# GQA decode attention: K transposes moved from TensorE to VectorE, a wide V accumulator, and load shapes that differ between the kv heads

## The chip, the cores and the metric

One core of a Trainium2 chip runs the whole program. The metric is the time of one execution on the device in microseconds (us). "The span" is the time from the first to the last instruction in a profiled execution. It is about 2 us shorter than the time.

Every run carries a state: fast, or slow when it lies over 1.5% above the fastest of the same kernel. One of the first two runs of the kernel before (745.04 us) was a slow one.

## The reference

```python
B, Hq, Hkv, Sq, Sk, D = 1, 32, 8, 1, 65536, 128      # bf16; q, k, v = normal * 0.05
k = jnp.repeat(k, Hq // Hkv, axis=1); v = jnp.repeat(v, Hq // Hkv, axis=1)
scores = jnp.einsum("bhqd,bhkd->bhqk", q, k) * D ** -0.5
out = jnp.einsum("bhqk,bhkd->bhqd", softmax(scores, -1), v)
```

There is one query token, 32 query heads, and 8 kv heads with 65536 keys each. K and V together are 268.4 MB and each byte is needed once. A kv head is 33.55 MB: four 4 MB K blocks and four 4 MB V blocks of 16384 keys.

## The kernel before

The scores need the head dimension on the partitions, but K arrives with the keys there. So each 128x128 chunk of K is transposed on TensorE into PSUM, copied to SBUF by VectorE, and used as the stationary operand of a matmul whose moving operand is four query columns. V needs no transpose: a V chunk is the stationary operand, and four columns of probabilities move.

```python
# io pool: 4 buffers of 4 MB, shared by K and V; all loads issued from SyncE
nc.sync.dma_start(out=kn, in_=k[0, g, block].rearrange("(c p t) d -> p c t d", p=P, t=32))  # 8 KB runs
# K step, a group of NW = 8 chunks
for i in range(NW):
    nc.tensor.transpose(out=pt[:, i*P:(i+1)*P], in_=kn[:, c, t0+i, :], identity=ident_bf)
nc.vector.tensor_copy(out=kTn, in_=pt)                       # 128x1024 bf16, PSUM -> SBUF
for i in range(NW):
    nc.tensor.matmul(out=sc[:, jj*4:(jj+1)*4], lhsT=kTn[:, i*P:(i+1)*P], rhs=qT_g)
# ... per head: max, exp on ScalarE, sum ...
# V step, one matmul for each chunk
nc.tensor.matmul(out=psum_oT, lhsT=vb[:, c, t, :], rhs=E_g[:, j*4:(j+1)*4])
# main loop: K groups of head g+1 alternate with V chunks of head g  [cut]
```

Of the kernel before, what the change touches and what calls it, by code (L numbers as in the profile page):

```python
# [13 lines left out]
IO_BUFS = int(os.environ.get("GQA_IOBUFS", "4"))  # L14
PTW = int(os.environ.get("GQA_PTW", "8"))
SBUFS = int(os.environ.get("GQA_SBUFS", "3"))
EBUFS = int(os.environ.get("GQA_EBUFS", "4"))
GRAN = int(os.environ.get("GQA_GRAN", "8"))
# [3 lines left out]
def kernel(  # L22
# [8 lines left out]
    P = nc.NUM_PARTITIONS  # L31
    B, Hq, Sq, D = q.shape
    _, Hkv, Sk, _ = k.shape
    assert B == 1 and Sq == 1 and D == P
    HPG = Hq // Hkv
    assert HPG * Hkv == Hq
    assert Sk % P == 0
    C = Sk // P
    SCALE = float(D) ** -0.5

    fp32 = mybir.dt.float32
    bf16 = mybir.dt.bfloat16

    KB = min(Sk, 16384)
    assert Sk % KB == 0
    NB = Sk // KB
    T = 32 if KB >= 32 * P else 1
    CB = KB // (P * T)
    CKB = KB // P
    assert CKB * HPG <= 512  # L50
    NW = PTW if T % PTW == 0 else 4
    assert CKB % GRAN == 0 and GRAN % NW == 0

    const = ctx.enter_context(tc.tile_pool(name="const", bufs=1))
    iopool = ctx.enter_context(tc.tile_pool(name="iopool", bufs=IO_BUFS))
    ktp = ctx.enter_context(tc.tile_pool(name="ktp", bufs=3))
    spool = ctx.enter_context(tc.tile_pool(name="spool", bufs=SBUFS))
    epool = ctx.enter_context(tc.tile_pool(name="epool", bufs=EBUFS))
    stats = ctx.enter_context(tc.tile_pool(name="stats", bufs=2))
    psc = ctx.enter_context(tc.tile_pool(name="psc", bufs=2, space=bass.MemoryType.PSUM))  # L60
    pst = ctx.enter_context(tc.tile_pool(name="pst", bufs=2, space=bass.MemoryType.PSUM))
    psm = ctx.enter_context(tc.tile_pool(name="psm", bufs=2, space=bass.MemoryType.PSUM))
    pso = ctx.enter_context(tc.tile_pool(name="pso", bufs=2, space=bass.MemoryType.PSUM))

    qT = const.tile([P, Hq], bf16)
    nc.sync.dma_start_transpose(out=qT[:, :], in_=q[0, :, 0, :])  # L66

    ident = const.tile([P, P], fp32)
    make_identity(nc, ident[:, :])
    ident_bf = const.tile([P, P], bf16)  # L70
    nc.vector.tensor_copy(out=ident_bf[:, :], in_=ident[:, :])
    ones_row = const.tile([1, P], fp32)
    nc.vector.memset(ones_row[:, :], 1.0)
    ones_mat = const.tile([P, P], fp32)
    nc.gpsimd.memset(ones_mat[:, :], 1.0)
    lsum_all = const.tile([P, Hq], fp32)
    rl_all = const.tile([P, Hq], fp32)
    oT_all = const.tile([P, Hq], bf16)

    E_tiles = [None] * Hkv  # L80
    S_tiles = [None] * Hkv
    psum_oTs = [None] * Hkv

    def stats_and_exp(g):
        S_g = S_tiles[g]
        S_view = S_g[:, :].rearrange("p (c h) -> p h c", h=HPG)
        mx = stats.tile([P, HPG], fp32, name="mx")
        nc.vector.tensor_reduce(out=mx[:, :], in_=S_view, axis=AX.X, op=ALU.max)  # L88
        psum_t = psm.tile([HPG, P], fp32, name="psum_t", tag="misc")
        nc.tensor.transpose(out=psum_t[:, :], in_=mx[:, :], identity=ident[:, :])  # L90
        m4 = stats.tile([HPG, 1], fp32, name="m4")
        nc.vector.reduce_max(out=m4[:, :], in_=psum_t[:, :], axis=AX.X)
        psum_mrow = psm.tile([1, HPG], fp32, name="psum_mrow", tag="misc")
        nc.tensor.transpose(out=psum_mrow[:, :], in_=m4[:, :], identity=ident[:HPG, :HPG])  # L94
        mrow = stats.tile([1, HPG], fp32, name="mrow")
        nc.vector.tensor_copy(out=mrow[:, :], in_=psum_mrow[:, :])  # L96
        psum_b = psm.tile([P, HPG], fp32, name="psum_b", tag="misc")
        nc.tensor.matmul(  # L98
            out=psum_b[:, :], lhsT=ones_row[:, :], rhs=mrow[:, :], start=True, stop=True
        )  # L100
        nmb = stats.tile([P, HPG], fp32, name="nmb")
        nc.vector.tensor_scalar_mul(out=nmb[:, :], in0=psum_b[:, :], scalar1=-SCALE)  # L102
        E_g = epool.tile([P, C * HPG], bf16, name="E_g")
        E_view = E_g[:, :].rearrange("p (c h) -> p h c", h=HPG)
        for h in range(HPG):
            nc.scalar.activation(  # L106
                out=E_view[:, h, :],
                in_=S_view[:, h, :],
                func=ACT.Exp,
                bias=nmb[:, h:h + 1],  # L110
                scale=SCALE,
                accum_out=lsum_all[:, g * HPG + h:g * HPG + h + 1],
            )
        E_tiles[g] = E_g
        psum_lb = psm.tile([P, HPG], fp32, name="psum_lb", tag="misc")
        nc.tensor.matmul(  # L116
            out=psum_lb[:, :],
            lhsT=ones_mat[:, :],
            rhs=lsum_all[:, g * HPG:(g + 1) * HPG],
            start=True,  # L120
            stop=True,
        )
        nc.vector.reciprocal(out=rl_all[:, g * HPG:(g + 1) * HPG], in_=psum_lb[:, :])  # L123

    class KBlock:
        def __init__(self, g, b):
            self.g = g
            self.b = b
            self.kn = iopool.tile([P, CB, T, D], bf16, name="kn", tag="io")
            nc.sync.dma_start(  # L130
                out=self.kn[:, :, :, :],
                in_=k[0, g, b * KB:(b + 1) * KB, :].rearrange("(c p t) d -> p c t d", p=P, t=T),
            )
            self.sc = psc.tile([P, CKB * HPG], fp32, name="sc")
            self.done = 0

        def step(self, nchunks):
            g = self.g
            qT_g = qT[:, g * HPG:(g + 1) * HPG]
            end = min(self.done + nchunks, CKB)  # L140
            while self.done < end:
                g0 = self.done
                c = g0 // T
                t0 = g0 % T
                pt = pst.tile([P, NW * P], bf16, name="pt")
                for i in range(NW):
                    t = t0 + i
                    nc.tensor.transpose(  # L148
                        out=pt[:, i * P:(i + 1) * P],
                        in_=self.kn[:, c, t, :],  # L150
                        identity=ident_bf[:, :],
                    )
                kTn = ktp.tile([P, NW * P], bf16, name="kTn")
                nc.vector.tensor_copy(out=kTn[:, :], in_=pt[:, :])  # L154
                for i in range(NW):
                    jj = g0 + i
                    nc.tensor.matmul(  # L157
                        out=self.sc[:, jj * HPG:(jj + 1) * HPG],
                        lhsT=kTn[:, i * P:(i + 1) * P],
                        rhs=qT_g,  # L160
                        start=True,
                        stop=True,
                    )
                self.done += NW
            if self.done >= CKB:
                S_g = S_tiles[g]
                c0 = self.b * CKB * HPG
                nc.vector.tensor_copy(out=S_g[:, c0:c0 + CKB * HPG], in_=self.sc[:, :])  # L168
                return True
            return False  # L170

    class VBlock:
        def __init__(self, g, b):
            self.g = g
            self.b = b
            self.vb = iopool.tile([P, CB, T, D], bf16, name="vb", tag="io")
            nc.sync.dma_start(
                out=self.vb[:, :, :, :],
                in_=v[0, g, b * KB:(b + 1) * KB, :].rearrange("(c p t) d -> p c t d", p=P, t=T),
            )  # L180
            if psum_oTs[g] is None:
                psum_oTs[g] = pso.tile([P, HPG], fp32, name="psum_oT")
            self.done = 0

        def step(self, nchunks):
            g = self.g
            E_g = E_tiles[g]
            psum_oT = psum_oTs[g]
            end = min(self.done + nchunks, CKB)
            while self.done < end:  # L190
                jj = self.done
                c = jj // T
                t = jj % T
                j = self.b * CKB + jj
                nc.tensor.matmul(  # L195
                    out=psum_oT[:, :],
                    lhsT=self.vb[:, c, t, :],
                    rhs=E_g[:, j * HPG:(j + 1) * HPG],
                    start=(j == 0),
                    stop=(j == C - 1),  # L200
                )
                self.done += 1
            if self.done >= CKB:
                if self.b == NB - 1:
# [5 lines left out]
                    )  # L210
                return True
            return False

    for g in range(Hkv):
        S_tiles[g] = spool.tile([P, C * HPG], bf16, name="S_g")

# [64 lines left out]
```

## Time and profile before

| Reading | Value | View |
|---|---|---|
| time, fast runs | about 708 us | run list |
| bytes from HBM at 426 GB/s, the rate of the best 20 us windows | 268.4 MB / 426 GB/s = 630 us | table by stage |
| one kv head, steady state | 87.8 us (382 GB/s) | packet records of the trace |
| TensorE | 12337 matmuls, 562 us busy | page, part 1 |

Lines of the page of the kernel before: busy time by engine; the span in 40 slices (digits are tenths busy, for PE and for DMA, then the rate of DMA); the chain of work that ended last; and the costliest groups (busy us, mean ns of one | idle time just before, and its releaser).

```profile
PE 562.4 (80%) x12337; PEld 505.3 (72%) x12337; DVE 396.7 (56%) x595; ACT 41.9 (6%) x65; POOL 0.8 (0%) x7
...
PE   1998898839988499884999849998498984999945
...
DMA  8999799997989979899799997989979899799994
GB/s 332 427 425 425 305 405 387 386 426 327 423 356 391 426 319 425 353 397 421 308 423 377 404 420 321 423 358 425 427 309 408 360 393 423 325 413 386 425 427 202
...
PE 67%; DVE 20%; issue 6%; ACT 5%; DMA 2%; SPq 0%; DVEq 0%; ACTq 0%
PE pt L148 34%; PE sc L157 17%; DVE kTn L154 15%; PE psum_oT L195 15%; ACT E_g L106 5%; DVE mx L88 3%; DMA kn<-in_k_dram 2%; DVE S_g L168 1%; PE psum_b L98 1%; PE psum_lb L116 1%; PE psum_t L90 0%; PE psum_mrow L94 0%; DVE nmb L102 0%; SPq 
...
L154 DVE COPY kTn<-pt 128x1024 bf16<-128x1024 bf16 x512 | 350.0, 691 | 223.1 <-PE pt L148 214.8
L148 PE MATMUL pt<-ident_bf,kn 128*128 128x128 bf16 x4096 | 367.5, 244 | 14.5 <-DMA kn<-in_k_dram 14.5
...
L157 PE MATMUL sc<-qT,kTn 128*128 128x4 bf16 x4096 | 184.1, 167 | 33.8 <-DVE kTn L154 18.2
...
L195 PE MATMUL psum_oT<-E_g,vb 128*128 128x4 bf16 x4096 | 118.7, 166 | 26.8 <-issue 26.8
```

The rate holds at 425 to 427 GB/s in the good slices and falls to between 305 and 327 in one slice of each head. The loads are the same in every slice, so the likely reading is that the stream is starved; experiment 1 tests it. The chain consists of TensorE and of the VectorE evictions between its transposes; DMA is 2% of it. Note that VectorE is idle for 223 us before the evictions, nearly all of it waiting for the PE transposes.

Table by stage, two windows of 20 us of the kernel before (columns: window, length, busy us of PE, PEld, DVE, ACT, POOL, then granted clock, DMA share, GB/s):

```profile
40.00:60.00 20.00, 17.89 (x392) 15.81 (x390) 17.24 (x27) 0.00 (x0) 0.00 (x0) 1.00 1.01 424
80.00:100.00 20.00, 18.89 (x420) 17.39 (x418) 13.38 (x22) 0.69 (x2) 0.00 (x0) 0.83 0.74 300
```

The first window is saturated (DMA share 1.01) while head 0 fills the buffers. In the second, TensorE is busy 18.89 of 20 us and DMA only 0.74. What the load queue waits for, in total over the span (us, times, longest):

```profile
SPq L130 <- PE psum_oT L195: 369.4, 20, 19.8
SPq L130 <- PE pt L148: 175.0, 8, 25.2
```

Loads wait for buffers that TensorE has not finished with. Two successive lines of the VectorE timeline in head 0 (start, busy us, of two groups each) give the pace of K work:

```profile
61.25 1.34 DVE L154 COPY kTn<-pt 128x1024 bf16<-128x1024 bf16 x2 [0.27 <-PE pt L148]
62.86 1.34 DVE L154 COPY kTn<-pt 128x1024 bf16<-128x1024 bf16 x2 [0.27 <-PE pt L148]
```

Two groups of eight chunks take 62.86 - 61.25 = 1.61 us, so a block of 16 groups takes 12.9 us, while a 4 MB block arrives in 9.8 us. From head 1 on, V work and the softmax come on top. In the timeline of VectorE, line L168 is the copy that closes a K block; here it is from the second block of one head to the second block of the next:

```profile
198.00 0.69 DVE L168 CAST S_g<-sc 128x512 bf16<-128x512 f32 x1 [0.47 <-PE sc L157]
218.02 0.69 DVE L168 CAST S_g<-sc 128x512 bf16<-128x512 f32 x1 [0.47 <-PE sc L157]
237.35 0.69 DVE L168 CAST S_g<-sc 128x512 bf16<-128x512 f32 x1 [0.40 <-PE sc L157]
263.24 0.69 DVE L168 CAST S_g<-sc 128x512 bf16<-128x512 f32 x1 [0.45 <-PE sc L157]
286.16 0.69 DVE L168 CAST S_g<-sc 128x512 bf16<-128x512 f32 x1 [0.47 <-PE sc L157]
```

One head takes 286.16 - 198.00 = 88.2 us, longer than the 78.7 us that its bytes need. Little of that is waiting for data: the K transposes waited 14.5 us for DMA in the whole span (line L148 above). The longest step, 25.9 us, contains the softmax. Two lines of the TensorE timeline show its end:

```profile
247.58 0.59 PE L116 MATMUL psum_lb<-lsum_all,ones_mat 128*128 128x4 f32 x2 [5.43 <-ACT E_g L106]
248.02 1.87 PE L148 MATMUL pt<-ident_bf,kn 128*128 128x128 bf16 x16
```

From the last scores (237.3 us) to the next K transposes (248.02 us) TensorE stands almost idle for 10.7 us; one head earlier it is 10.6 us (149.6 to 160.2 us).

### The profile page before, as it was taken

What the parts mean: (1) busy time and instruction counts of PE and PEld (TensorE: products, weight loads), DVE (VectorE), ACT (ScalarE), POOL (GpSimd) and SP (SyncE); (2) the same over time, 40 slices, a digit from 0 to 9 for tenths busy, and PEclk for the clock granted to TensorE, in tenths of its full rate; (3) what the DMA queues carried; (4) which work ended last, traced back from release to release, by engine and by line L of the source; (5) the groups of instructions that cost most, each with busy time, mean ns of one, the idle gap of its engine ahead of it and who ended that gap; (6) DMA issues with size and microseconds to landing.
All of it is one profiled execution on the core that took longest, in us unless ns stands there. A gap on an engine that the chain in (4) does not pass through costs nothing.

```text
span 705.8 us, 26009 instructions
## 1 busy us (share of the span) xinstructions
PE 562.4 (80%) x12337; PEld 505.3 (72%) x12337; DVE 396.7 (56%) x595; ACT 41.9 (6%) x65; POOL 0.8 (0%) x7
## 2 busy tenths in 40 slices
PE   1998898839988499884999849998498984999945
PEld 1777887738877388773888738888387873888845
DVE  1888666536565365653656536566265662656620
ACT  0000200020000200002000020000200002000020
POOL 0000000000000000000000000000000000000000
PEclk9999788868988678876788768788578885789755
DMA  8999799997989979899799997989979899799994
GB/s 332 427 425 425 305 405 387 386 426 327 423 356 391 426 319 425 353 397 421 308 423 377 404 420 321 423 358 425 427 309 408 360 393 423 325 413 386 425 427 202
DMA packets 34011, 270.12 MB, mean 383 GB/s; under 512 B 1136, under 2 KB 1136, under 8 KB 1136
## 3 DMA queue, kind: packets, MB, share of 16 engines
q1 hardware_dynamic: 33904, 268.46, 91.9%
q8 instruction: 96, 1.57, 0.8%
q14 instruction: 11, 0.09, 0.0%
HBM read 268.44 MB, written 0.01 MB: 380 GB/s over the span
## 4 chain that ended last, share of the span: by engine, by line
PE 67%; DVE 20%; issue 6%; ACT 5%; DMA 2%; SPq 0%; DVEq 0%; ACTq 0%
PE pt L148 34%; PE sc L157 17%; DVE kTn L154 15%; PE psum_oT L195 15%; ACT E_g L106 5%; DVE mx L88 3%; DMA kn<-in_k_dram 2%; DVE S_g L168 1%; PE psum_b L98 1%; PE psum_lb L116 1%; PE psum_t L90 0%; PE psum_mrow L94 0%; DVE nmb L102 0%; SPq L66 0%; DVE mrow L96 0%
## 5 line engine op out<-in xcount | busy, mean ns | idle before, releaser
L154 DVE COPY kTn<-pt 128x1024 bf16<-128x1024 bf16 x512 | 350.0, 691 | 223.1 <-PE pt L148 214.8
L148 PE MATMUL pt<-ident_bf,kn 128*128 128x128 bf16 x4096 | 367.5, 244 | 14.5 <-DMA kn<-in_k_dram 14.5
L148 PEld LDWEIGHTS <-kn 128*128 128x128 bf16 x4096 | 281.6, 109 | 14.5 <-DMA kn<-in_k_dram 14.5
L157 PE MATMUL sc<-qT,kTn 128*128 128x4 bf16 x4096 | 184.1, 167 | 33.8 <-DVE kTn L154 18.2
L157 PEld LDWEIGHTS <-kTn 128*128 128x128 bf16 x4096 | 145.8, 99 | 84.2 <-DVE kTn L154 75.9
L195 PE MATMUL psum_oT<-E_g,vb 128*128 128x4 bf16 x4096 | 118.7, 166 | 26.8 <-issue 26.8
L195 PEld LDWEIGHTS <-vb 128*128 128x128 bf16 x4096 | 114.2, 99 | 28.8 <-issue 28.8
L106 ACT ACTIVATE E_g<-S_g,nmb 128x512 bf16<-128x512 bf16 x32 | 40.6, 1416 | 641.0 <-DVE nmb L102 641.0
L116 PE MATMUL psum_lb<-lsum_all,ones_mat 128*128 128x4 f32 x16 | 4.4, 349 | 37.9 <-ACT E_g L106 37.9
L116 PEld LDWEIGHTS psum_lb<-lsum_all,ones_mat 128*128 128x128 f32 x16 | 3.8, 295 | 38.6 <-ACT E_g L106 38.6
L168 DVE CAST S_g<-sc 128x512 bf16<-128x512 f32 x32 | 22.1, 690 | 12.5 <-PE sc L157 12.5
L123 DVE RECIPROCAL rl_all<-psum_lb 128x4 f32<-128x4 f32 x8 | 1.5, 181 | 40.5 <-PE psum_lb L116 40.5
L90 PE MATMUL psum_t<-ident,mx 128*4 128x128 f32 x8 | 2.9, 360 | 23.2 <-DVE mx L88 23.2
L88 DVE TENSOR_REDUCE mx<-S_g 128x4 f32<-128x2048 bf16 x8 | 18.3, 2284 | 0.2
L90 PEld LDWEIGHTS psum_t<-ident,mx 128*4 128x4 f32 x8 | 0.6, 81 | 23.9 <-DVE mx L88 22.3
L205 DVE TENSOR_TENSOR oT_all<-psum_oT,rl_all 128x4 bf16<-128x4 f32 x8 | 1.2, 153 | 18.1 <-PE psum_oT L195 18.1
L106 ACT ACTIVATION_READ_ACCUMULATOR E_g<-S_g,nmb 128x1 f32 x32 | 8.0, 251 | 0.0
L98 PE MATMUL psum_b<-mrow,ones_row 1*128 1x4 f32 x16 | 4.7, 361 | 1.7 <-DVE mrow L96 1.7
L98 PEld LDWEIGHTS psum_b<-mrow,ones_row 1*128 1x128 f32 x16 | 4.0, 308 | 2.4 <-DVE mrow L96 2.3
L102 DVE TENSOR_SCALAR nmb<-psum_b 128x4 f32<-128x4 f32 x8 | 1.3, 163 | 5.3 <-PE psum_b L98 5.2
L96 DVE COPY mrow<-psum_mrow 1x4 f32<-1x4 f32 x8 | 1.2, 150 | 1.9 <-PE psum_mrow L94 1.8
L106 ACT ACT_TABLE_LOAD x1 | 1.3, 1283 | 0.7 <-PEq L265 0.7
(36 smaller groups left out, 6.2 us busy)
## 6 DMA issues: line engine op xcount, KB each, us to landing
kn<-in_k_dram SPq DMA_DIRECT2D x32, 4096.0 KB, 14.0
vb<-in_v_dram SPq DMA_DIRECT2D x32, 4096.0 KB, 23.1
qT<-in_q_dram SPq DMA_TRANSPOSE x1, 2.3
out_dram<-o_sb SPq DMA_DIRECT2D x1, 8.0 KB, 1.4
```

What stands on the lines that cost most here:

```text
L88: nc.vector.tensor_reduce(out=mx[:, :], in_=S_view, axis=AX.X, op=ALU.max)
L90: nc.tensor.transpose(out=psum_t[:, :], in_=mx[:, :], identity=ident[:, :])
L98: nc.tensor.matmul(out=psum_b[:, :], lhsT=ones_row[:, :], rhs=mrow[:, :], start=True, stop=True)
L102: nc.vector.tensor_scalar_mul(out=nmb[:, :], in0=psum_b[:, :], scalar1=-SCALE)
L106: nc.scalar.activation(out=E_view[:, h, :], in_=S_view[:, h, :], func=ACT.Exp, bias=nmb[:, h:h + 1], scale=SCALE, accum_out=lsum_all[:, g ...
L116: nc.tensor.matmul(out=psum_lb[:, :], lhsT=ones_mat[:, :], rhs=lsum_all[:, g * HPG:(g + 1) * HPG], start=True, stop=True,)
L123: nc.vector.reciprocal(out=rl_all[:, g * HPG:(g + 1) * HPG], in_=psum_lb[:, :])
L148: nc.tensor.transpose(out=pt[:, i * P:(i + 1) * P], in_=self.kn[:, c, t, :], identity=ident_bf[:, :],)
L154: nc.vector.tensor_copy(out=kTn[:, :], in_=pt[:, :])
L157: nc.tensor.matmul(out=self.sc[:, jj * HPG:(jj + 1) * HPG], lhsT=kTn[:, i * P:(i + 1) * P], rhs=qT_g, start=True, stop=True,)
L168: nc.vector.tensor_copy(out=S_g[:, c0:c0 + CKB * HPG], in_=self.sc[:, :])
L195: nc.tensor.matmul(out=psum_oT[:, :], lhsT=self.vb[:, c, t, :], rhs=E_g[:, j * HPG:(j + 1) * HPG], start=(j == 0), stop=(j == C - 1),)
```

## The change

VectorE transposes K directly from SBUF to SBUF, as pairs: two adjacent bf16 are seen as one 32-bit word, and 128x2048 words are transposed in 32x32 squares. The odd layout that results is absorbed in the stationary operand, a zero-padded copy of the query (`wz`), so that 32 matmuls of 512 moving columns give all scores of a block, already in one PSUM tile. V uses 16 probability columns as the stationary operand and 512 V columns as the moving one. Of each 16x512 result only the diagonal blocks are wanted; a mask and a reduction take them out once a head. Four column strips of the array are used in turn. In addition the kv heads load with different descriptor sizes or from different queues (heads 0 and 7 alike). The diff is condensed to its core, with long expressions shortened.

```diff
-    transpose on TensorE, eviction on VectorE, matmul of 4 columns (above)
+SHAPE = [(32768, "sp"), (16384, "sp"), (8192, "sp"), (4096, "sp"), (2048, "sp"),
+         (32768, "alt"), (32768, "pool"), (32768, "sp")]     # per kv head
+    view = src[0, g, block].rearrange("(p t) d -> p t d", p=P)          # 32 KB runs
+    e.dma_start(out=t[:, lo:hi, :], in_=view[:, lo:hi, :], max_dma_last_dim=piece)
+    for t0 in range(0, SL, TS):                              # TS = 32, four in a block
+        nc.vector.transpose(out=kt, in_=kn[:, t0:t0+TS, :]...bitcast(u32))   # 128x2048 words
+        for u in range(0, TS, 16):
+            for s in range(2):
+                for w in range(2):
+                    nc.tensor.matmul(out=sc, lhsT=wz[:, g, s, w, 28-4*gp:28-4*gp+P],
+                                     rhs=ktb[:, u:u+16, s, :, w])            # 512 columns
+    mx = max over each sc tile; softmax as before; probabilities transposed on VectorE
+    for tt in range(16):                                     # twice in a V block
+        c = tt % 4
+        nc.tensor.matmul(out=vacc[32*c:32*c+16, 0:512], lhsT=et[:, b, o:o+16],
+                         rhs=vt[... 4 chunks ...])                           # 512 columns
+    # after a head: vacc * mask, reduce, one small matmul  [cut]
-    K of head g+1 and V of head g interleaved
+    K of head g, softmax, V of head g, K of head g+1, in this order
+    last V block loaded in pieces of 64, 32, 16, 8, 8 chunks
```

## The prediction

> **What bounds the kernel now.** The page shows a span of 705.8 us. 268.4 MB of K and V must come from HBM. In the table by stage, 20 us windows with the DMA share at 1.01 moved 424 to 426 GB/s (8 KB packets), so a stream that never starves would need 268.4 MB / 426 GB/s = 630 us. The remaining 76 us are starvation: windows around the turn from one kv head to the next fall to 300-340 GB/s, because the queue waits for buffers (the queue's own waits: 369 us on the V matmuls, 175 us on the K transposes). TensorE frees those buffers late: the chain of waits is 67% PE (K transposes 34%, scores 17%, V 15%) and 15% VectorE evictions. PE is busy 562 us with 12337 matmuls (244 ns per transpose, 166 ns per 4-column matmul) at a mean granted clock of 0.786. It is a nearly balanced DMA/PE kernel, exposed about 10 us per head.
>
> **What the change does.** It removes 4096 PE transposes, 512 evictions (691 ns), the score copies and 8192 narrow matmuls. Added, per 4 MB K block: 4 VectorE transposes of 128x2048 32-bit words. Estimate from the 2048-element reduction in the trace (2284 ns, one element per cycle): 2.28 us each, 9.1 us a block, plus a 512-element max of about 0.7 us: 9.8 us, just the 9.84 us in which a block arrives. PE: 32 matmuls of 512 columns per block; the Trainium skill ("TensorE: Matmul & The Clock Gate", Back-to-back issue gap) gives about 216 ns warm, so 7 us a block, an estimate no run here shows. V matmuls target four column strips and may overlap.
>
> **Critical path.** Serial compute loop of a head: K transposes 39 us, last scores and softmax about 6, V matmuls at most 28, collection 2: about 75 us, against 78.7 us of DMA for 33.5 MB. Four buffers are freed well before they are needed. So DMA should become the bound nearly everywhere, and the starvation between heads vanish.
>
> **Descriptors.** The skill ("Advanced Engine Details and Errata", Clock Domains) gives 42 to 43 ns for an unobstructed 1 KiB descriptor. This trace's 8 KB packet takes 8192 B x 16 / 426 GB/s = 308 ns; together: about 5 ns fixed per descriptor. Estimate per head: 32 KB 77.5 us, 16 KB 78, 8 KB 78.6, 4 KB 80, 2 KB 82. Sum 629. ScalarE or GpSimd issuing should cost little (the skill's DMA page, "Issuing engines are not separate DMA queues"), allow 4 us. Start about 4 us (before's first load issued at 1.97 us), tail about 5 us (last piece's landing, small matmuls, store), launch difference 1 us.
>
> **Predicted: 643 us, 8-in-10 range 632 to 682.** Chance of faster by over 2%: 0.95; within 2%: 0.02; slower: 0.03.
>
> **What would show it right.** DMA share near 1.0 in all slices but the first and last, 405-430 GB/s, lowest in the 2 KB head (slices 21-25); VectorE transposes near 2.3 us; queue waits long before each issue but DMA never idle; chain of waits mostly DMA; PE under 75% busy.
>
> **What would make it wrong.** 32-bit transposes at half rate (4.4 us): K phase 75 us, head about 95 us, 770 us in all. Strided moving reads slowing the score matmuls, or a low granted clock, stretching the serial loop past 79 us. GpSimd descriptor writing or ScalarE's in-order queue (its V loads are behind a K wait in that head) leaving gaps of several us. Large descriptors being less efficient than assumed. Before's two runs differ by 5%, so its median may overstate the gain.

## The result and the profile after

The changed kernel took 651.17 us (650.98 and 651.36), correct, against 725.97 us, the median of a fast and a slow run of the kernel before. The ratio is 0.9205 (95% interval 0.9154 to 0.9256). A ratio is taken from fast runs of the same rounds, so it is not quite the ratio of the medians quoted.

The page of the changed kernel, the lines that answer to those above:

```profile
PE 371.9 (57%) x2136; PEld 146.4 (23%) x2136; DVE 355.5 (55%) x291; ACT 24.4 (4%) x65; POOL 9.4 (1%) x15
...
PE   0776537673476734767348562248834767247674
...
DMA  9999999999999999999999999999999999999995
GB/s 386 424 419 449 417 424 430 424 431 419 422 420 419 420 416 410 409 410 408 404 387 386 386 387 417 407 434 425 436 429 428 433 432 427 429 436 429 426 434 231
...
DMA 45%; PE 25%; DVE 17%; issue 13%; ACT 0%; POOL 0%; ACTq 0%; SPq 0%; POOLq 0%; DVEq 0%
DMA kn<-in_k_dram 25%; PE sc L128 21%; DMA vt<-in_v_dram 18%; DVE kt L119 14%; PE vacc L186 2%; DMA q_in<-in_q_dram 1%; DVE mx L141 1%; ACT e L165 0%; DVE et L169 0%; PE fin L231 0%; DVE wz L107 0%; POOL vt L60 0%; PE pb L155 0%; ACTq L66 0
...
L128 PE MATMUL sc<-kt,wz 128*128 128x512 bf16 x1024 | 270.3, 421 | 126.8 <-DVE kt L119 126.8
L119 DVE STREAM_TRANSPOSE kt<-kn 128x2048 uint32<-128x2048 uint32 x128 | 284.3, 2278 | 46.5 <-DMA kn<-in_k_dram 46.5
...
L186 PE MATMUL vacc<-vt,et 128*16 128x512 bf16 (+1 forms) x1024 | 90.5, 517 | 122.7 <-DMA vt<-in_v_dram 107.8
```

The DMA share is at 9 tenths or more in every slice but the last, which is the tail. TensorE's matmuls are down from 12337 to 2136 and its busy time from 562 to 372 us; VectorE's is down from 397 to 356 us. Now look at the rates, counting slices from 0: mostly 417 to 431 over the first heads, 408 to 410 in slices 15 to 18, 386 to 387 in slices 20 to 23, and about 430 from slice 26 on. These steps follow the list of load shapes. The packet records of the trace give the time in which each 33.55 MB landed:

| Head | Load shape | predicted us | measured us | GB/s |
|---|---|---|---|---|
| 0 | 32 KB, SyncE (with the start) | 77.5 | 79.3 | 423 |
| 1 | 16 KB, SyncE | 78 | 78.5 | 428 |
| 2 | 8 KB, SyncE | 78.6 | 79.9 | 420 |
| 3 | 4 KB, SyncE | 80 | 82.1 | 409 |
| 4 | 2 KB, SyncE | 82 | 85.9 | 390 |
| 5 | 32 KB, SyncE and ScalarE | 77.5 | 79.5 | 422 |
| 6 | 32 KB, GpSimd | 77.5 | 78.0 | 430 |
| 7 | 32 KB, SyncE (with the tail's pieces) | 77.5 | 79.3 | 423 |
| sum | | 629 | 642.3 | |

Two things in this profile mislead. First, the queue still waits for buffers; two lines of the load queue's waits after:

```profile
SPq L60 <- DVE kt L119: 224.7, 22, 11.4
SPq L60 <- DMA vt<-in_v_dram: 113.1, 7, 78.1
```

These waits are harmless: loads issued earlier keep DMA full meanwhile. Second, the chain names TensorE and VectorE for over 40% of the span, although DMA is never idle. Here the compute and the stream hand each other buffers and data in turn, and the chain goes through whichever released last. The DMA share of the slices is the reading that decides.

The timeline of one head, from its first K block to that of the next head (start, length, engine, line, count, [idle before <- releaser]):

```profile
92.50 8.89 DVE L119 STREAM_TRANSPOSE kt<-kn 128x2048 uint32<-128x2048 uint32 x4 [3.97 <-DMA kn<-in_k_dram]
...
104.05 0.69 DVE L141 TENSOR_REDUCE mx<-sc 128x1 f32<-128x512 f32 x1 [2.66 <-PE sc L128]
104.66 8.88 DVE L119 STREAM_TRANSPOSE kt<-kn 128x2048 uint32<-128x2048 uint32 x4
...
130.28 8.51 PE L128 MATMUL sc<-kt,wz 128*128 128x512 bf16 x32 [3.00 <-DVE kt L119]
138.83 0.69 DVE L141 TENSOR_REDUCE mx<-sc 128x1 f32<-128x512 f32 x1 [2.02 <-PE sc L128]
...
142.91 2.30 PE L186 MATMUL vacc<-vt,et 128*16 128x512 bf16 x24 [1.87 <-DVE et L169]
...
151.32 1.90 PE L186 MATMUL vacc<-vt,et 128*16 128x512 bf16 x32 [3.08 <-DMA vt<-in_v_dram]
...
161.14 3.24 PE L186 MATMUL vacc<-vt,et 128*16 128x512 bf16 x32 [7.92 <-DMA vt<-in_v_dram]
...
171.08 2.31 DVE L119 STREAM_TRANSPOSE kt<-kn 128x2048 uint32<-128x2048 uint32 x1 [4.09 <-DMA kn<-in_k_dram]
```

A head takes 171.08 - 92.50 = 78.6 us. Three of these lines carry waits for data: 3.08 us and 7.92 us for V, 4.09 us for the next K. The remaining 63.5 us are work in series, against 88.2 us for a head before. Part of the difference is the softmax: from the end of the last scores (138.8 us) to the first V matmul (142.91 us) it is now 4.1 us, where the kernel before had 10.7 us. The text of the change does not list this, and no experiment tried it by itself.

### The profile page after: what moved, and what is told of

The parts are those of the page before. It is cut to its first block, busy times and chain, and to the rows that moved or that the text cites. A ratio compares the mean times of both kernels' runs of the same rounds, so it can differ in the third digit from the quotient of the medians.

```text
span 649.2 us, 4927 instructions
## 1 busy us (share of the span) xinstructions
PE 371.9 (57%) x2136; PEld 146.4 (23%) x2136; DVE 355.5 (55%) x291; ACT 24.4 (4%) x65; POOL 9.4 (1%) x15
## 3 DMA queue, kind: packets, MB, share of 16 engines
q0 software_dynamic: 1152, 33.55, 12.0%
## 4 chain that ended last, share of the span: by engine, by line
DMA 45%; PE 25%; DVE 17%; issue 13%; ACT 0%; POOL 0%; ACTq 0%; SPq 0%; POOLq 0%; DVEq 0%
DMA kn<-in_k_dram 25%; PE sc L128 21%; DMA vt<-in_v_dram 18%; DVE kt L119 14%; PE vacc L186 2%; DMA q_in<-in_q_dram 1%; DVE mx L141 1%; ACT e L165 0%; DVE et L169 0%; PE fin L231 0%; DVE wz L107 0%; POOL vt L60 0%; PE pb L155 0%; ACTq L66 0%; DVE m L147 0%
## 5 line engine op out<-in xcount | busy, mean ns | idle before, releaser
L128 PE MATMUL sc<-kt,wz 128*128 128x512 bf16 x1024 | 270.3, 421 | 126.8 <-DVE kt L119 126.8
L119 DVE STREAM_TRANSPOSE kt<-kn 128x2048 uint32<-128x2048 uint32 x128 | 284.3, 2278 | 46.5 <-DMA kn<-in_k_dram 46.5
L128 PEld LDWEIGHTS <-wz 128*128 128x128 bf16 x1024 | 106.3, 104 | 289.3 <-issue 196.1
L186 PE MATMUL vacc<-vt,et 128*16 128x512 bf16 (+1 forms) x1024 | 90.5, 517 | 122.7 <-DMA vt<-in_v_dram 107.8
L186 PEld LDWEIGHTS <-et 128*16 128x16 bf16 (+1 forms) x1024 | 33.4, 111 | 171.8 <-issue 146.4
L141 DVE TENSOR_REDUCE mx<-sc 128x1 f32<-128x512 f32 x32 | 21.9, 689 | 62.6 <-PE sc L128 62.6
L165 ACT ACTIVATE e<-sc,nmb 128x512 bf16<-128x512 f32 x32 | 21.7, 683 | 601.6 <-DVE nmb L160 600.8
L169 DVE STREAM_TRANSPOSE et<-e 128x512 bf16<-128x512 bf16 x32 | 22.1, 711 | 8.6 <-ACT e L165 8.6
L203 DVE TENSOR_REDUCE vs<-vm 128x128 f32<-128x512 f32 x8 | 8.2, 1020 | 0.2
L165 ACT ACTIVATION_READ_ACCUMULATOR e<-sc,nmb 128x1 f32 x32 | 6.2, 195 | 0.0
L246 PEld LDWEIGHTS fin<-vs,sel 128*4 128x4 f32 x14 | 0.6, 84 | 15.5 <-DVE vs L203 15.5
## 6 DMA issues: line engine op xcount, KB each, us to landing
vt<-in_v_dram SPq DMA_DIRECT2D x25, 4096.0 KB, 27.9
vt<-in_v_dram POOLq DMA_DIRECT2D x4, 4096.0 KB, 27.9
```

The source lines that it names most:

```text
L119: nc.vector.transpose(out=kt[:, :], in_=kn[:, t0:t0 + TS, :].rearrange("p t d -> p (t d)").bitcast(u32),)
L128: nc.tensor.matmul(out=sc[:, :], lhsT=wz[:, g, s, w, 28 - 4 * gp:28 - 4 * gp + P], rhs=ktb[:, u:u + 16, s, :, w], start=(n == 0), stop=(n ...
L141: nc.vector.tensor_reduce(out=mx[:, b:b + 1], in_=scs[b][:, :], axis=AX.X, op=ALU.max)
L165: nc.scalar.activation(out=e[:, :], in_=scs[b][:, :], func=ACT.Exp, bias=nmb[:, :], scale=SCALE, accum_out=ls[:, b:b + 1],)
L169: nc.vector.transpose(out=et[:, b, :], in_=e[:, :])
L186: nc.tensor.matmul(out=vacc[32 * c:32 * c + 4 * ng, 0:ng * D], lhsT=et[:, b, o:o + 4 * ng], rhs=vt[:, :, :].rearrange("p (y t) d -> p y t ...
```

## The experiments

All twelve gave results that the comparison with the reference calls correct. Each has three timed rounds beside the kernel before on the same chip. The theories are: **A**, the kernel before is starved because its K work, softmax and V work in series take longer than a head's bytes, and the change removes that; **B**, the load shapes carry the gain; **C**, there are too few buffers.

### 1. Half of the K transposes, in the kernel before

```diff
-                pt = ...; 8 transposes; kTn = ...; tensor_copy(kTn, pt)
+                if (g0 // NW) % 2 == 0:
+                    pt = ...; 8 transposes; kTn = ...; tensor_copy(kTn, pt); self.kTn = kTn
+                kTn = self.kTn
```

> Kernel before, with every second group of eight K transposes and its VectorE eviction left out (the scores of that group reuse the previous group's transposed keys, so the result is wrong on purpose; loads, score matmuls, softmax and V part are unchanged). Theory A (before is starved because the K transposes on PE and their evictions make a head take 88 us, more than the 79 us its bytes need): half of 367 us of PE transposes gone, the head drops well under 79 us, the stream saturates and the span falls to 640-655 us. Rival B (the load shape, 8 KB packets or the queue, limits before): unchanged, about 706 us. Rival C (too few buffers, whatever the PE work): mostly unchanged, above 690 us.

Measured: 654.16 us, ratio 0.9233 (0.9219 to 0.9248). The scores are wrong on purpose; the comparison still passed, so this comparison does not see such an error. Lines of the page:

```profile
DMA  8999999999999999999999999999999999999982
GB/s 323 428 423 425 426 424 424 427 426 425 424 427 424 426 425 426 424 425 427 425 423 425 427 423 427 425 424 426 426 423 425 425 427 425 424 426 424 426 364 114
```

The dips are gone and the stream is saturated, with the loads of the kernel before untouched. One line of its load queue's waits:

```profile
SPq L130 <- PE pt L149: 313.8, 28, 15.7
```

The wait for the transposes is longer than in the kernel before (175 us), yet it no longer costs anything. Three things differ together: PE work, evictions, and the granted clock, which was 1.0 in this run and 0.79 before. So it shows that taking work off the K path is enough to end the starvation, not which of the three counts most. A higher clock is not needed: the changed kernel saturates the stream at 0.81. Two things remain untested: the softmax stretch, which this run leaves in place and the change shortens, might by itself have brought part of the gain, and the new order of K, softmax and V was not tried alone.

### 2. A fifth buffer, in the kernel before

```diff
-IO_BUFS = 4
+IO_BUFS = 5
```

> Kernel before with five 4 MB load buffers in place of four. Theory A (too much PE work per head): a fifth buffer only lets the queue run 10 us further ahead once; 695-706 us. Rival C (the queue starves because buffers are too few at the turn of a head): the dips to 300-340 GB/s go and the time falls towards 640-660 us.

Measured: 706.11 us, ratio 0.9949 (0.9914 to 0.9984). C falls: heads 2 to 7 still take 86 to 89 us, and only the first turn is smoother. Six buffers were not tried.

### 3. 32 KB descriptors, in the kernel before

```diff
-    T = 32
+    T = 128          # 32 KB runs for each partition
```

> Kernel before with 32 KB runs per partition in place of 8 KB, nothing else. Theory A: 700-708 us, since the stream waits for buffers, not for descriptors. Rival B (load shape is the gain): falls to 650 us or so.

Measured: 717.46 us, ratio 1.0133 (1.0081 to 1.0184), so not faster, and a little slower, also than the 700 to 708 us expected. B falls for this kernel. The edit also changes which keys share a partition; why it is slower was not tried.

### 4. 32 KB from SyncE in all heads of the changed kernel

```diff
-SHAPE = [eight different]
+SHAPE = [(32768, "sp")] * 8
```

> Changed kernel with 32 KB descriptors from the SyncE queue in all eight heads. Theory A with a fixed cost of 8 ns per descriptor (a line through the head times of the changed kernel, 78.0 us at 32 KB to 85.9 us at 2 KB): 8 x 78.1 us + 9 us of start, tail and launch = 634 us, 17 us under the changed kernel. If the head times were set by something else that drifts over the execution (the 2 KB head lies in the middle), the middle heads stay slow and the time stays at 648-652 us.

Measured: 635.69 us, ratio 0.8975 (0.8958 to 0.8992). The rates over the span:

```profile
GB/s 366 433 435 430 432 433 435 432 429 427 433 433 430 433 430 431 435 430 429 430 435 431 427 431 427 435 430 433 431 430 433 430 431 433 427 431 430 431 427 238
```

Every inner head takes 77.8 to 78.0 us. So the mixed list cost 15.5 us, and the slow middle was due to the shapes, not to the place in the execution.

### 5. 2 KB and 1 KB in all heads

```diff
+SHAPE = [(2048, "sp")] * 8      # and, as another kernel, [(1024, "sp")] * 8
```

> Changed kernel, 2 KB descriptors from SyncE in all heads. A line through the head times of the changed kernel gives 8.2 ns fixed + 36.9 ns per KB for each descriptor on its engine, 85.9 us a head: 8 x 85.9 + 9 = 696 us. With the 5 ns of the prediction, 82 us a head: 665 us. If the 2 KB head was slow only because of its place in the execution: about 640 us.

Measured: 706.79 us, ratio 0.9985 (0.9936 to 1.0034). This is above all three expectations, and it gives back the whole gain of the change. Inner heads take 86.9 us. The 85.9 us that I used was the 2 KB head with its edges, where loads of other shapes overlap; the rate of its inner slices, 386 to 387 GB/s, already said 86.8 us.

> Changed kernel, 1 KB descriptors from SyncE in all heads. The line, used outside the sizes it was fitted on: 46.0 ns a descriptor, 16384 of them on each of 16 engines, 754 us + 9 = 763 us. The skill's 42 to 43 ns for an unobstructed 1 KiB descriptor: 696 + 9 = 705 us. If making the descriptors on the queue sets a second limit that 2 KB does not reach: above 780 us.

Measured: 783.49 us, ratio 1.1071 (1.1007 to 1.1136), 96.5 us a head. The rates show how flat the bound is:

```profile
GB/s 305 348 348 348 348 348 348 348 348 348 348 348 348 348 348 348 349 347 348 348 348 348 348 348 348 348 348 348 348 348 348 348 348 348 348 348 348 348 348 234
```

The descriptor times follow from the uniform runs. A head in 2 KB is 1024 descriptors on each of 16 engines, 86.9 us / 1024 = 84.9 ns; in 32 KB it is 64 descriptors, 77.94 us / 64 = 1218 ns. The line through both has 37.8 ns per KB and 9.3 ns fixed. It gives 47.1 ns for 1 KB, and 96.5 us / 2048 = 47.1 ns was measured; it gives 312 ns for 8 KB, and 79.9 us / 256 = 312 ns was measured (experiment 9). So there is no second limit down to 1 KB. The miss at 1 KB (763 expected, 783 measured) is mostly the error of the earlier line, which had 8.2 ns fixed and so 46.0 ns at 1 KB: 1.1 ns on 16384 descriptors is 18 us. Its slope was the same, since the 36.9 ns in the expectation for 2 KB are per 1000 bytes and the 37.8 ns here per 1024.

### 6. Other issuing queues in all heads

```diff
+SHAPE = [(32768, "pool")] * 8   # and, as another kernel, [(32768, "alt")] * 8
```

> Changed kernel, 32 KB descriptors, all loads issued by GpSimd. If the issuing engine costs nothing once the queue runs ahead (78.0 us in the GpSimd head of the changed kernel): within 3 us of the same kernel with SyncE, 633-639 us. If descriptor writing in software leaves gaps: over 642 us.

> Changed kernel, 32 KB descriptors, blocks alternating between SyncE and ScalarE. The alternating head of the changed kernel took 79.5 us against 78.0 us, with windows of 397 GB/s at the hand-over. If that is a cost of each head (a load behind a wait in ScalarE's in-order queue): 8 x 1.5 = 12 us over SyncE alone, about 647 us. If it came only from the change of shape at that head: 635-638 us.

Measured: GpSimd 636.86 us (ratio 0.8994, 0.8951 to 0.9038), alternating 634.78 us (0.8968, 0.8923 to 0.9013), against 635.69 us from SyncE alone. The queue is free here, within what these runs resolve. Alternating heads take 77.8 to 78.1 us here, so the 79.5 us of head 5 in the changed kernel is no cost of alternating as such. The hand-over between two arrangements is left as the likely cause; it was not tried by itself.

### 7. One column strip for the V matmuls

```diff
-            c = tt % 4
+            c = 0
-                stop=last and tt >= 12,
+                stop=last and tt >= 15,
```

> Changed kernel with all V matmuls in one column strip of the array in place of four in turn. If the four strips run at the same time now (3.6 us for the 32 matmuls of a block): they become serial, 7 to 8 us a block, V matmul time on the engine about twice. Theory of slack (a V block has 9.8 us, and the profile shows a wait of 25 us for K at each turn of a head): the time stays at 650-653 us. The prediction's reading (serial loop of a head only 4 us short of the stream): 14 us more a head than measured now, 680 us or more only if the loop really is that tight.

Measured: 664.49 us, ratio 0.9376 (0.934 to 0.941). Neither expectation was right: 13 us slower. The stream is as before until its end. Windows of the changed kernel, then of this one, at the end of the span:

```profile
640.00:650.00 10.00, 4.61 (x62) 3.45 (x53) 2.06 (x3) 0.00 (x0) 0.00 (x0) 0.76 0.25 99
```

```profile
640.00:650.00 10.00, 10.00 (x48) 4.14 (x46) 0.00 (x0) 0.00 (x0) 0.00 (x0) 1.00 0.25 99
650.00:660.00 10.00, 6.47 (x62) 4.29 (x60) 2.06 (x3) 0.00 (x0) 0.00 (x0) 1.00 0.00 0
```

In both kernels the same 99 GB/s flow between 640 and 650 us and nothing after. Here TensorE is still busy with V all through that window and into the next. The matmuls after the first few of the last head, in one line of the timeline:

```profile
629.31 25.00 PE L186 MATMUL vacc<-vt,et 128*16 128x512 bf16 x121
```

These 121 matmuls (16 of them of 256 columns) take 25.0 us, 221 ns for each 512 columns. In the changed kernel the 32 matmuls of a block take 1.90 to 3.59 us, so 7.1 us in one strip against that is a gain of 2 to 3.7 times from the strips. In every head but the last this hides under the stream. In the last head the V work starts at about 627 us and the data end at about 644 us. Four blocks need 28 us in one strip, so they end at 654 us, 10 us behind the data; with four strips they end just behind the data. The profiled run is the fastest of this kernel's four, and its span is 10.7 us longer than the changed kernel's, so that is where the loss lies; the slower runs have no profile. I had treated the head as periodic and forgotten its last instance.

### 8. One more transpose in each K block

```diff
+            if t0 == 0:
+                nc.vector.transpose(out=spare, in_=kn[:, t0:t0+TS, :]...bitcast(u32))
```

> Changed kernel with one more VectorE transpose of 128x2048 in each K block (five in place of four, the fifth into a spare tile), 2.28 us x 4 = 9.1 us more VectorE work a head. The prediction's reading, a serial loop of 75 us against 78.7 us: 84 us a head, about 40 us slower, 690 us. Slack of about 25 us a head, as the wait for K at each turn shows: no change, 650-654 us.

Measured: 652.53 us, ratio 0.921 (0.9188 to 0.9233): no change. But the experiment is weaker than planned. Its timeline:

```profile
114.61 0.66 DVE L148 TENSOR_REDUCE mx<-sc 128x1 f32<-128x512 f32 x1
...
115.18 2.30 DVE L120 STREAM_TRANSPOSE kt<-kn 128x2048 uint32<-128x2048 uint32 x1
```

In the changed kernel each max waits 2.0 to 2.7 us for the last score matmuls, in order on VectorE, and the next transposes wait behind it (the lines at 104.05 and 138.83 us above). With the extra transpose the scheduler places the max behind two transposes of the next block, where the scores are ready. The K phase of this head grew from 47.0 to 48.6 us, not by 9.1 us. So the run shows that VectorE had unused time in its K phase; it does not measure the slack of a head. The 25 us in the expectation was also a misreading: it was the length of DMA pieces in the chain, while the waits of the head shown sum to 15 us.

### 9. The narrow V form, and 8 KB in all heads

```diff
-    wide(...); collect(...)
+    for t in range(SL):     # one matmul of 128 columns for each chunk
+        nc.tensor.matmul(out=fin, lhsT=et[:, b, o:o+4], rhs=vt[:, t, :])
```

> Changed kernel with the wide accumulator undone: every V chunk is one matmul of 128 columns into a 4x128 accumulator, 4096 in place of 1024, no mask and no collection. The K part is kept. If the wide accumulator is part of the gain: slower by over 5 us. If the stream alone sets the time and the K part made the gain: 648-654 us, with V matmuls of 5 to 8 us a block on the engine.

Measured: 665.27 us, ratio 0.9387 (0.9361 to 0.9414), so 14 us slower; the run was expected to be level. V takes about 7.3 us a block (490 matmuls in 27.9 us at the end), and the loss is again mainly in the tail: DMA moves 2 GB/s between 650 and 660 us while TensorE is busy all 10 us. The wide accumulator is worth about 14 us, and it is the four strips that make it so.

For the V part of the kernel before, the timeline has, for a whole block of V:

```profile
690.53 3.57 PE L195 MATMUL psum_oT<-E_g,vb 128*128 128x4 bf16 x128 [1.63 <-issue]
```

That is the upper end of the wide form's 1.90 to 3.59 us. On the engine the wide form gains little over the old V step, then; it keeps V that cheap in the new layout.

> Changed kernel with the 8 KB descriptors of the kernel before, from SyncE, in all heads: the computing part of the change alone. Line through the head times: 8 x 79.9 + 9 = 648 us, that is 60 us of the 57 us gain over before from the computing part and nothing from the load shapes. If load shapes carried some of the gain it would be slower than the changed kernel (651 us) by more than 5 us.

Measured: 651.27 us, ratio 0.9198 (0.9176 to 0.922). With the descriptor size of the kernel before, the computing part alone gives 57 us of 708 us. The mixed list happens to average out at the same time as 8 KB. In experiment 1 the same size took 79.2 to 79.4 us a head in the address order of the kernel before; why it takes 79.9 us here is open.

## Why the prediction was right

The time (643 predicted, 632 to 682 as range, 651.17 measured) and the reason held. Point by point:

- **"The remaining 76 us are starvation"**: right. Halving the K transposes alone saturated the stream (experiment 1), while a buffer more (2) or larger descriptors (3) did not.
- **"2.28 us each"** for the VectorE transposes: right, 2278 ns measured. The estimate came from a reduction of 2048 elements in the trace before, 2284 ns.
- **"about 216 ns warm"** for 512 columns: 221 ns in experiment 7, where nothing else paces them. The section of the Trainium skill that the prediction cites ("TensorE: Matmul & The Clock Gate", Back-to-back issue gap) gives this figure for an isolated matmul and says that it is too high for a stream of them; the prediction left that out, and the 221 ns of a stream in one strip side with its figure. In the changed kernel they are paced by the transposes, 8 in 2.2 us.
- **"K transposes 39 us", "V matmuls at most 28 us", loop "about 75 us"**: the sum was too pessimistic and two terms were off in opposite directions. The K phase is 47 us, since each max waits 2 us for TensorE in VectorE's order, which I missed. V takes half or less of 28 us thanks to the strips. Without its waits the loop is 63.5 us in the head shown, 15 us under the stream.
- **Descriptors, "about 5 ns fixed"**: the mis-sized term. Measured 9.3 ns fixed with 37.8 ns per KB, so the eight heads took 642 us instead of 629. The measured line alone gives 639 us for them, so about 10 of the 13 us are this term; the rest is at the edges of heads 0, 5 and 7. All-32 KB at 635.69 us shows that the shapes, and no compute, hold the changed kernel above it.
- **"allow 4 us" for other queues**: not needed; all three are within 0.4% of each other.
- **"start about 4 us", "tail about 5 us", "launch difference 1 us"**: fair in sum. The span is 649.2 us around 642.3 us of stream, and the time is 1.8 us over the span. Of these allowances, 14 us with the queues, 8.7 us were used; the other 5.3 us hid part of the 13 us that the stream was off. That the time came out within 8 us is to that extent luck.
- **"chain of waits mostly DMA"**: only 45%, although DMA is the bound. The test was badly chosen; the DMA share was the good one.

The version that beats both kernels is the change with 32 KB descriptors everywhere, 634.8 to 636.9 us whatever the queue, about 10% under the kernel before.

## What to carry to other kernels

Divide the bytes by the best rate that the trace itself shows, and compare the serial work of one period with it: if work exceeds it, take work off the path (a buffer more and larger descriptors did nothing for the kernel here); once work fits, the descriptor size is what was left here, and 2 KB returned the whole gain. Waits of a load queue for buffers cost nothing while the DMA share stays full. What hides under the stream in every period is bare in the last one, so cost the tail separately.

## What the Trainium skill lacked or had wrong

- "DMA: Bandwidth & Descriptors", Specifications, gives 512 B and up as the least transfer for line rate. From HBM with one core's stream saturated, the rate still depended on size well above that: 348 GB/s at 1 KB, 386 at 2 KB, 409 at 4 KB (one head), 420 at 8 KB, 428 at 16 KB (one head), 430 at 32 KB. A fixed cost of a descriptor measured at these sizes, 9.3 ns here, is on no page; the same page, Why small descriptors are slow, states a fixed overhead of about 3 cycles per packet, with 256 B as its example.
- "Advanced Engine Details and Errata", Clock Domains, has 42 to 43 ns for an unobstructed 1 KiB descriptor. In a saturated stream of 1 KB descriptors it took 47.1 ns, so the figure is too low to plan a stream with.
- "VectorE: DVE Perf Modes", The three transpose paths, has a 128x128 bf16 figure only. A transpose of 128x2048 32-bit words took 2278 ns and one of 128x512 bf16 took 711 ns, that is 4096 bf16 of a partition in 2278 ns as pairs against 512 in 711 ns singly.
- "DMA: Bandwidth & Descriptors", Issuing engines are not separate DMA queues: nothing wrong, as far as these runs go: 634.8, 635.7 and 636.9 us for three arrangements.
